# The first batch in two token halves, with its values mixed and transposed on chip, and experts run on one half while the other is prepared

**Chip, cores, metric.** One core of one Trainium2 chip. The metric is the device time of one execution in microseconds (us).

## The reference

A block attention feeds a mixture of four experts. What matters of it:

```python
# attention: q, k, v are [4, 8, 768, 64]; sort_net is [4, 8, 8, 8]
P = sort_net
for _ in range(5):                         # normalisation loop
    P = exp(P - P.max(-1)); P /= P.sum(-1); P /= P.sum(-2)
k_sorted = einsum('bhij,bhjcd->bhicd', P, k_blocks)      # mixes the 8 blocks of 96 tokens
v_sorted = einsum('bhij,bhjcd->bhicd', P, v_blocks)
attn = softmax(q_blocks @ k_sorted^T / 8);  attn_out = attn @ v_sorted   # within a block
# experts: x = attn_out as [3072, 512]; w1 [4, 512, 1024], w2 [4, 1024, 512]
p = domain_probs / domain_probs.sum(-1)
out = sum_e p[:, e] * (relu(x @ w1[e]) @ w2[e])
```

## The kernel before

Everything is fp16 for the matmuls. The 128 partitions of a loaded tensor hold 8 blocks x 16 tokens, so mixing the blocks is a matmul with a matrix built from the mixing weights and a mask (`PIk`, `PIv`). Mixed keys come out transposed, as scores need them. Mixed values come out with the wrong tokens on the partitions, and a trip through DRAM puts that right. Attention of batch b+1 is put as "filler" between the expert matmuls of batch b; attention of batch 0 runs alone, ahead of everything. Cut to what the change and the argument touch:

```python
for lo in range(0, H, 4):
    for nm in ("k", "v", "q"):
        load_natural(0, nm, lo, 4)                 # GpSimd queue, fp32 -> fp16
ident = const.tile([P, P], F16); make_identity(nc, ident)
nc.vector.tensor_reduce(eye16[:], ident..., AX.X, ALU.max)      # masks on VectorE
nc.vector.tensor_copy(maskk..., eye16...); nc.vector.tensor_copy(maskv..., eye16...)
...
load_w1(0); load_w2(0)
for it in range(5):                                # normalisation loop: ACT exp, then six DVE ops
    ...
nc.vector.tensor_copy(sn16[:], ...)                # broadcast, 1024 elements
for i in range(NB): nc.tensor.matmul(ps_R[:, i, :], sn16[:, i]..., ident[0:GH, 0:GH])
build_PI(nc.vector, 0, "v"); build_PI(nc.vector, 0, "k")
build_PI(nc.gpsimd, 1, "v"); build_PI(nc.gpsimd, 1, "k")
load_w1(1); load_w2(1)
for nm in ("k", "v", "q"): load_natural(1, nm, 0, H)
for n in range(2, GH // 4): build_PI(nc.gpsimd, n, "v"); build_PI(nc.gpsimd, n, "k")
for e in range(2, E): load_w1(e); load_w2(e)

def st_v(b, pr):                                   # mix the values of a head pair
    ...
    if pr % 2:                                     # after each four heads: through DRAM
        nc.sync.dma_start(vs_dram[b, qd]..., vo...)
        nc.sync.dma_start(vs..., vs_dram[b, qd]...)

for f in attention_order(0): f()                   # batch 0 alone
mix_weights()                                      # p_sb = p / sum(p), four DVE ops
for b in range(B):
    ...
    experts(b, attention_order(b + 1) if b + 1 < B else [])
```

The profiles name an instruction by the tiles that it writes and reads. Names that begin with `ps_` are tiles in PSUM: `ps_R` holds the mixing weights, `ps_k` and `ps_v` mixed keys and values (`ps_mk` and `ps_mv` in the changed kernel), `ps_q` transposed queries, `ps_s` scores, `ps_a` attention outputs with their row sums, `ps_x` these outputs transposed, `ps_h` and `ps_o` the first and second product of an expert. Their copies in SBUF are `kT`, `vo` (`vT` in the changed kernel), `qT`, `ET` (exponentials of the scores), `xsl` (normalised outputs), `xT` (input of the experts) and `hT`; `vs` are the values as attention needs them. In the changed kernel `ps_w` is the tile of the warm-up matmuls and also that of the transposed values.

Buffers in PSUM: two pools of two 4 KiB tiles. During batch 0 attention uses all four in turn; afterwards the experts have one pool and attention the other.

The softmax here doesn't subtract the row's maximum and nothing guards it: scores larger than these inputs give would overflow.

## Time and profile before

| | before |
|---|---|
| time, median (lowest to highest) | 431.98 us (431.8 to 432.4, 3 runs) |
| span of the profiled execution | 429.6 us |
| busy: PE / PEld / DVE / ACT / POOL | 387.3 / 212.8 / 155.4 / 128.3 / 35.1 us |
| first expert matmul on the chain | 56.79 us |
| one expert on one batch (64 + 48 matmuls) | 10.40 + 10.36 us |

PE is the TensorE, PEld its weight loads, DVE the VectorE, ACT the ScalarE, POOL the GpSimd. A PE that is 90% busy says little by itself; where the other 10% lies says more. The view of waits, for PE in the whole execution (engine, line, releaser, us in total, times, longest), puts it in two places, both at the start:

```profile
PE ps_R L158 <- DVE sn L152: 16.4, 1, 16.4
PE ps_a L288 <- DMA vs<-vs_dram: 16.2, 2, 15.7
```

The first is the wait for the normalisation loop, the second the wait for values that come back from DRAM. The prediction shows the chain and the timeline of this stretch.

### The profile page before, as it was taken

Reading aid. Unit: us, or ns where it says so; the run is one execution under the profiler, and the core shown is the slowest. Engines: PE = TensorE matmul, PEld = TensorE weight load, DVE = VectorE, ACT = ScalarE, POOL = GpSimd, SP = SyncE. Lnnn points to the kernel's source line nnn. Section 1 sums busy time; section 2 is a strip of 40 time slices with the busy share of each in tenths; the row PEclk is TensorE's granted clock in tenths of the full one; section 3 lists DMA queues with packets and bytes.
Section 4 is the critical chain, followed back from the end, with each engine's and each line's share of the span. In section 5 each row is a group of like instructions: output and inputs, shape, how many; then the busy total and the mean of one; then the engine's idle time right before and its main releaser. Section 6 shows DMA issues by size and latency. Waiting matters only on the chain.

```text
span 429.6 us, 6396 instructions
## 1 busy us (share of the span) xinstructions
PE 387.3 (90%) x2856; PEld 212.8 (50%) x2856; DVE 155.4 (36%) x265; ACT 128.3 (30%) x166; POOL 35.1 (8%) x51
## 2 busy tenths in 40 slices
PE   0321889999999999999999999999999999999995
PEld 0211655554646555555646454555556454545552
DVE  3831643434243434334253424343352403030312
ACT  1010323241605232351506041432406050514140
POOL 6396200000011000000000000000000000000000
PEclk9975569999999999999999999999999999999999
DMA  9999999940009422200000221200000300000003
GB/s 133 207 211 227 226 209 211 223 105 2 2 0 183 111 76 77 76 2 0 2 2 2 98 78 48 77 2 0 2 2 0 125 23 2 0 2 0 0 26 123
DMA packets 30027, 31.07 MB, mean 72 GB/s; under 512 B 1584, under 2 KB 24112, under 8 KB 30000
## 3 DMA queue, kind: packets, MB, share of 16 engines
q0 software_dynamic: 18800, 17.83, 25.5%
q1 hardware_dynamic: 11200, 12.84, 9.6%
q8 instruction: 22, 0.36, 0.3%
q14 instruction: 5, 0.04, 0.0%
HBM read 38.95 MB, written 9.54 MB: 113 GB/s over the span
## 4 chain that ended last, share of the span: by engine, by line
PE 86%; DMA 7%; DVE 4%; POOL 1%; issue 1%; ACT 0%; SPq 0%; POOLq 0%
PE ps_h L365 40%; PE ps_o L379 39%; DMA vs_dram<-vo 5%; PE ps_a L288 2%; DMA vs<-vs_dram 1%; PE ps_x L310 1%; PE ps_q L238 1%; PE ps_k L250 1%; PE ps_s L267 1%; PE ps_v L210 1%; DVE xsl L297 1%; DVE vo L217 0%; POOL nat_k L84 0%; POOL nat_v L84 0%; DVE PIk L173 0%
## 5 line engine op out<-in xcount | busy, mean ns | idle before, releaser
L365 PE MATMUL ps_h<-xT,w 128*128 128x384 f16 x1024 | 177.8, 329 | 0.0
L371 ACT ACTIVATE hT<-ps_h 128x768 f16<-128x768 f32 x128 | 103.8, 811 | 237.8 <-PE ps_h L365 237.8
L379 PE MATMUL ps_o<-w,hT 128*128 128x512 f16 x768 | 171.9, 379 | 0.0
L365 PEld LDWEIGHTS <-w 128*128 128x128 f16 x1024 | 97.9, 99 | 65.6 <-issue 2.2
L379 PEld LDWEIGHTS <-hT 128*128 128x128 f16 x768 | 73.6, 98 | 85.1
L390 DVE SCALAR_TENSOR_TENSOR oacc<-ps_o,p_sb,oacc 128x512 f32<-128x512 f32 x72 | 54.1, 751 | 104.9 <-PE ps_o L379 104.9
L274 ACT ACTIVATE ET<-ps_s 96x768 f16<-96x768 f32 x32 | 24.0, 802 | 37.8 <-PE ps_s L267 37.8
L386 DVE TENSOR_SCALAR oacc<-ps_o,p_sb 128x512 f32<-128x512 f32 x24 | 18.0, 751 | 34.5 <-PE ps_o L379 34.5
L288 PE MATMUL ps_a<-vs,ET 96*128 96x65 f16 x256 | 12.0, 206 | 16.2 <-DMA vs<-vs_dram 16.2
L297 DVE TENSOR_TENSOR xsl<-ps_a,rz 96x512 f16<-96x512 f32 x32 | 22.0, 687 | 1.1
L217 DVE CAST vo<-ps_v 128x768 f16<-128x768 f32 x16 | 15.1, 950 | 17.6 <-PE ps_v L210 17.6
L313 DVE COPY xT<-ps_x 128x768 f16<-128x768 f16 x16 | 8.9, 556 | 34.2 <-PE ps_x L310 34.2
L257 DVE CAST kT<-ps_k 128x768 f16<-128x768 f32 x16 | 15.2, 953 | 15.4 <-PE ps_k L250 15.2
L288 PEld LDWEIGHTS <-ET 96*128 96x128 f16 x256 | 11.1, 106 | 18.6 <-issue 16.0
L296 DVE RECIPROCAL rz<-ps_a 96x8 f32<-96x8 f32 x32 | 6.3, 197 | 34.3 <-PE ps_a L288 34.3
L242 DVE COPY qT<-ps_q 128x768 f16<-128x768 f16 x16 | 8.8, 551 | 19.3 <-PE ps_q L238 19.3
L158 PE MATMUL ps_R<-ident,sn 32*128 32x32 f16 x8 | 0.4, 185 | 16.4 <-DVE sn L152 16.4
L310 PE MATMUL ps_x<-ident,xsl 96*128 96x96 f16 x128 | 9.3, 224 | 3.6 <-DVE xsl L297 3.6
L84 POOL DMA_DIRECT2D nat_k<-in_k_dram x5 | 4.3, 868 | 85.9 <-PE ps_k L250 85.1
L310 PEld LDWEIGHTS <-xsl 96*128 96x128 f16 x128 | 7.9, 107 | 6.3 <-DVE xsl L297 4.4
L267 PE MATMUL ps_s<-qT,kT 64*128 64x96 f16 x256 | 9.5, 222 | 0.3 <-DVE kT L257 0.2
L210 PE MATMUL ps_v<-nat_v,PIv 128*128 128x384 f16 x32 | 8.8, 375 | 1.0 <-DVE PIv L180 1.0
(41 smaller groups left out, 89.2 us busy)
## 6 DMA issues: line engine op xcount, KB each, us to landing
w<-in_moe_w_dram POOLq DMA_DIRECT2D x8, 1024.0 KB, 20.9
out_dram<-oacc SPq DMA_DIRECT2D x24, 256.0 KB, 2.0
vs_dram<-vo SPq DMA_DIRECT2D x8, 396.0 KB, 6.5
vs<-vs_dram SPq DMA_DIRECT2D x8, 396.0 KB, 3.6
nat_k<-in_k_dram POOLq DMA_DIRECT2D x3, 768.0 KB, 23.3
nat_v<-in_v_dram POOLq DMA_DIRECT2D x3, 768.0 KB, 27.9
nat_q<-in_q_dram POOLq DMA_DIRECT2D x3, 768.0 KB, 30.7
nat_k<-in_k_dram POOLq DMA_DIRECT2D x2, 384.0 KB, 6.6
```

The lines of the kernel that those rows point to most:

```text
L217: nc.vector.tensor_copy(vo[:, :, ds(2 * (pr % 2), 2), 0:D], ps[:, :, 0:R * D].rearrange("p h (r d) -> p r h d", r=R),)
L257: nc.vector.tensor_copy(kT[:, 0:S].rearrange("p (i r c) -> p i r c", i=NB, r=R), ps.rearrange("p r (i c) -> p i r c", c=CP),)
L267: nc.tensor.matmul(pss[hh][:, i // HB, ds((i % HB) * BLK, BLK)], kT[ds(D * hh, D), ds(i * BLK, P)], qT[ds(D * hh, D), i, :], start=True, s ...
L274: nc.scalar.activation(ETs[2 * (pr % 2) + hh][:, 0:S].rearrange("c (a x) -> c a x", a=2), pss[hh][0:BLK, :, 0:HS], AF.Exp, bias=0.0, scale ...
L288: nc.tensor.matmul(ps[:, i // HB, ds((i % HB) * VW, D + 1)], ET[:, ds(i * BLK, P)], vs[:, i, 2 * (pr % 2) + hh, 0:D + 1], start=True, stop ...
L297: nc.vector.tensor_tensor(xsl[:, :, hh, :].rearrange("c (a i) d -> c a i d", a=2), av[:, :, :, 0:D], rz[:].broadcast_to([BLK, 2, HB, D]), ...
L310: nc.tensor.transpose(ps[:, i, :], xsl[:, i, :, :].rearrange("c h d -> c (h d)"), ident[0:BLK, 0:BLK])
L365: nc.tensor.matmul(ps[:, nh, 0:HS], w1sb[e][:, kc, ds(fc * P, P)], xT[:, kc, ds(nh * HS, HS)], start=(kc == 0), stop=(kc == NKC - 1),)
L371: nc.scalar.activation(hT[:, fc, :].rearrange("p (a x) -> p a x", a=2), ps[:, :, 0:HS], AF.Relu, bias=0.0, scale=1.0,)
L379: nc.tensor.matmul(ps[:], hT[:, fc, ds(r * P, P)], w2sb[e][:, fc, :], start=(fc == 0), stop=(fc == NFC - 1),)
L386: nc.vector.tensor_scalar(out=oacc[r][:], in0=ps[:], scalar1=pcol, scalar2=None, op0=ALU.mult)
L390: nc.vector.scalar_tensor_tensor(out=oacc[r][:], in0=ps[:], scalar=pcol, op0=ALU.mult, in1=oacc[r][:], op1=ALU.add,)
```

## The change

The intent is to shorten the stretch before the experts. Batch 0 is cut into two halves of 384 tokens (four of the eight blocks each). Only the first half is prepared ahead; its values are mixed into transposed form, copied out of PSUM, and turned by TensorE transposes (`h_w`) instead of by DRAM. (The functions `q_half`, `h_k`, `h_v`, `h_w`, `h_s`, `h_a` and `h_x` are the units of one half: queries, mixed keys, mixed values, transposed values, scores, attention outputs, transposed outputs.) The experts 0 and 1 then run on that half while the second half is prepared as filler. Smaller parts: masks and their reduction move to GpSimd, identity comes after two loads instead of six, 76 warm-up matmuls on the identity go before the loop's result is there, the broadcast copy is shared by DVE and ACT, and loads are reordered. The core of the diff:

```diff
-    for lo in range(0, H, 4):
-        for nm in ("k", "v", "q"):
-            load_natural(0, nm, lo, 4)
+    load_natural(0, "k", 0, 4)
+    load_natural(0, "q", 0, 4, 0, P // 2)          # 64 partitions = first half of q
     ident = const.tile([P, P], F16, name="ident")
     make_identity(nc, ident)
+    load_natural(0, "v", 0, 4)
+    load_natural(0, "k", 4, 4)
+    load_natural(0, "v", 4, 4)
+    load_natural(0, "q", 4, 4, 0, P // 2)
+    load_natural(0, "q", 0, H, P // 2, P // 2)
-    nc.vector.tensor_reduce(eye16[:], ident..., AX.X, ALU.max)
-    nc.vector.tensor_copy(maskk..., eye16...)
+    nc.gpsimd.tensor_copy(eye16[:], ident[:, 0:CP])
+    for j in range(1, NB):
+        nc.gpsimd.tensor_tensor(eye16[:], eye16[:], ident[:, ds(j * CP, CP)], ALU.add)
+    nc.gpsimd.tensor_copy(maskk..., eye16...)
 ...
+    warm(28)                                        # matmuls of the identity
+    for pr in range(2):
+        q_half(0, pr, 0, nc.scalar.copy)
+    warm(48)
 ...
+    def h_w(qd, hf):                                # values: transposes instead of DRAM
+        for n in range(2 * HB):
+            nc.tensor.transpose(ps[:, n, :], vT[:, ds(n * BLK, BLK)], ident[:])
+        nc.vector.tensor_copy(vs0s[qd]..., ps...)
 ...
-    for f in attention_order(0):
-        f()
+    h_k(0, 0); h_v(0, 0)                            # (first half, one call a line)
+    for pr in range(2, 4): q_half(0, pr, 0, nc.scalar.copy)
+    h_k(1, 0); h_s(0, 0); h_w(0, 0); h_v(1, 0)
+    ...
+    h_s(1, 0); h_a(0, 0); h_w(1, 0); h_x(0, 0, ...); h_a(1, 0); h_x(1, 0, ...)
     mix_weights()
+    second = [q_half 0, h_k 0, h_v 0, q_half 1, h_k 1, h_s 0, h_w 0, h_v 1,      # of half 1
+              q_half 2, h_a 0, q_half 3, h_w 1, h_s 1, h_x 0, h_a 1, h_x 1]
+    run([(0, 0, 0), (0, 1, 0)], second, 2)          # (batch, expert, half)
+    run([(0, 0, 1), (0, 1, 1), (0, 2, 0), (0, 2, 1), (0, 3, 0), (0, 3, 1)], attention_order(1))
+    for b in range(1, B):
+        ...
+        run([(b, e, None) for e in range(E)], attention_order(b + 1) if b + 1 < B else [])
```

## The prediction

> **What bounds the kernel now.** I read the busy slices of the page first (10.7 us each), then the chain that ended last in order of time, then the timeline of the first 60 us, then the DMA issues one by one.
>
> ```profile
> PE   0321889999999999999999999999999999999995
> PEclk9975569999999999999999999999999999999999
> DMA  9999999940009422200000221200000300000003
> ```
>
> From the sixth slice on the TensorE (PE) has no idle time; before it, it is mostly empty. The kernel is a start of some 56 us that waits for something else, and then one dense run of matmuls. The chain says the same:
>
> ```profile
> 20.96 13.06 DMA vs_dram<-vo
> 34.45 9.93 DMA vs_dram<-vo
> 44.40 5.91 DMA vs<-vs_dram
> ...
> 56.79 5.99 PE ps_h L365 x24
> ...
> 82.07 1.30 PE ps_h L365 x8
> 83.81 2.71 PE ps_h L365 x16
> ...
> 92.84 0.49 PE ps_a L288 x16
> ...
> 341.99 10.40 PE ps_h L365 x64
> ...
> 414.67 10.37 PE ps_o L379 x48
> 425.07 0.75 DVE oacc L390
> ```
>
> Columns: start, duration, what. The mixed values of batch 0 go to DRAM and back (vs_dram, vs); from 20.96 to 50.3 us this path is all that the chain holds. The first expert matmul that counts starts at 56.79, the last ends at 425.07: 368.3 us. One expert on one batch is 10.40 (ps_h, 64 matmuls) + 10.36 (ps_o, 48) = 20.76 us, so sixteen are 332.2. The other 36.1 us are attention work for batches 1 to 3 put between. The gap between two expert pieces gives a unit's price: 83.37 to 83.81, 0.44 us for the score matmuls of a head pair. By expert groups the four batches start at 56.79, 153.25, 247.62 and 341.99, so attention costs 94.4 - 83.0 = 11.3 us a batch; the first has 2.1 us more, because its first 24 matmuls took 5.99 us where later ones take 3.90: the TensorE was still at half clock. The end, 425.07 to 429.6, is 4.5 us; the measured time is 2.4 us above the span.
>
> The start itself, from the timeline:
>
> ```profile
> 2.40 0.26 ACT L140 ACTIVATE sn<-sn 32x64 f32<-32x64 f32 x1 [0.38 <-DMA sn<-in_sort_net_dram]
> 6.47 0.38 DVE L109 TENSOR_REDUCE eye<-ident 128x16 f16<-128x128 f16 x1 [6.47 <-POOL ident masks.py:199]
> 7.13 0.20 DVE L141 TENSOR_REDUCE srow<-sn 32x8 f32<-32x64 f32 x1
> 8.88 0.21 DVE L141 TENSOR_REDUCE srow<-sn 32x8 f32<-32x64 f32 x1 [0.32 <-ACT sn L140]
> 15.63 0.68 DVE L152 CAST sn<-sn 32x1024 f16<-32x1024 f32 x1
> 40.19 1.04 PE L288 MATMUL ps_a<-vs,ET 96*128 96x65 f16 x16 [15.69 <-DMA vs<-vs_dram]
> ```
>
> The first exponential of the normalisation loop is done at 2.66, but VectorE (DVE), in order, sits at the mask that needs the identity until 6.47, so the loop starts at 7.13 and ends at 15.6: 8.47 us for five rounds of 1.755.
>
> **What the Trainium skill says.** (1) "TensorE: Matmul & The Clock Gate", Part 1: The HAM clock gate: the array runs at half clock until about 3.4 us of sustained activity, and falls back after an idle window. The trace agrees where the granted clock shows it: 0.50 from 30 to 57 us, and the 5.99 against 3.90 us above. Its 1.00 for 16 to 24 us I don't believe: the four ps_v matmuls there (384 columns) stand 0.32 us apart, which is half speed. (2) "DMA: Bandwidth & Descriptors", Queues, rings and completion order: each DMA engine takes turns between queues packet by packet, so a store on the SyncE queue shares with weight loads. The trace agrees: the 396 KB store took 13.1 and 9.9 us while about 210 GB/s flowed, against a median of 6.5. (3) "PSUM — Partial Sum Buffer", Specifications: 8 banks of 2 KiB. Two pools of two 4 KiB tiles fill them, so attention units placed between experts have two buffers in turn; the trace of before has no such wait in its dense part, and the change places them more tightly.
>
> **The change part by part.**
>
> *Masks to GpSimd (POOL).* DVE is free when the exponential is done. The loop starts at 2.7 and ends at 2.7 + 8.5 = 11.2: 4.4 us earlier. The broadcast copy is halved over two engines: 0.4 instead of 0.68. Then four ps_R matmuls (0.3) and one 512-element product from PSUM (about 0.7): mixing can start near 12.6. The added warm-up matmuls lie before it in otherwise idle TensorE time; at full clock 48 of 128 columns cost 2.6 us, at half 5.1, so they end near 12 either way. Keys land at 6.2 and the rest of batch 0 by 15.9, as in before: each 384 KB load landed 1.95 us after the one ahead.
>
> *Half of batch 0 ahead of the experts, without DRAM.* The serial path, with rows of before for each copy: keys of four heads mixed on TensorE (24 short matmuls, 0.7) to 13.3; values to 14.0; ScalarE (ACT) evicts vT (0.81) to 14.9; q transposes; second keys to 15.6, evicted by DVE (0.95) to 16.6; scores from 15.6 to 16.2; exponentials (0.80 each), behind two q copies, to 17.8; value transposes 16.2 to 16.7, evicted by DVE (1024 f16, about 0.75 from 556 ns for 768) to 17.5; second values, ACT copy to 18.6; ps_a from 18.1; DVE two times 0.20 + 0.69 to 20.4; vs of the second four heads to 21.2; ps_a; again two normalisations to 23.5; transposes 0.45; ACT copy 0.81 to 24.8. So the dense run starts near 25.3 instead of 56.8. Weights of expert 0 are no earlier limit: w1 landed at 20.8 and w2 at 24.0 in before, after the same bytes. I add 1.0 us, half of the 2.1, for an even chance of a cold first stretch: 26.3.
>
> *The other half becomes filler.* By matmul count against units of before: four q halves (0.3 each) 1.3, four mixings of 24 matmuls (0.75) 3.0, two value transposes 0.7, two scores 0.9, two ps_a 1.0, two ps_x 0.7: 7.5 us of TensorE time, moved into the dense run, not removed.
>
> *Waits of these fillers.* Sixteen units go into twelve slots of 1.3 to 1.7 us, with two buffers. Scores directly after a key mixing wait for its 0.95 us eviction: 1.0. ps_a directly after a q half waits for an accumulation (0.75) and the q copy: 0.9. ps_x directly after scores waits for ACT (a relu and an exponential): 1.2. Others 0.9. Sum 4.0. Batch 1 has its 24 units in 38 slots instead of 50: 0.6.
>
> *Expert work.* Halves use 384 columns as before; matmul count and price stay: 332.2. Attention of batches 1 to 3: 33.9.
>
> Sum: 26.3 + 332.2 + 7.5 + 4.0 + 0.6 + 33.9 + 4.5 = 409.0 us of span; plus 2.4 is 411.4 us. I say **411**, 4.9% below 432.0. In differences: -30.5 for the start, -2.1 for the cold stretch counted inside it, +7.5 for the moved work, +4.6 for waits.
>
> **The rivals.** *The loads become the bound.* At about 200 GB/s, batch 0 and four weight matrices are landed by about 32 us, batch 1 by 44, the last weights by about 62. Expert 1 needs its first matrix at about 40, batch 1's attention starts near 59, expert 2 near 87. All have 8 us or more in hand, so I give this 10%; it would make the time 415 to 422. *The store and load of batch 1's values starve ps_a.* The bounce still exists there. It starts near 62 us, ps_a follows some 24 us later; even the 19 us of the contended first bounce fits. If not, +5. *TensorE stays cold through the start*: at half clock each short unit on the path costs 0.2 to 0.3 us more, some 2 us, and the first experts 2 us: 414. *Fillers stall harder*: if every unit of batch 0's second half waits about 1 us, waits are 12 instead of 4: 419. *Better*: if fillers overlap with evictions as smoothly as in before, and the start is at 24: 405.
>
> **Range and chances.** The start may be 2.5 us off either way, the filler waits -3 to +6; together 404 to 419 for 8 in 10. To lose the 2% (423.3) most of the rivals would have to come together: faster 0.95, same 0.04, slower 0.01.
>
> **What would show it.** First dense ps_h near 25 us; no DMA in the chain before it, but alternating PE, ACT and DVE; the normalisation loop ending near 11.2; TensorE idle 3 to 6 us between 26 and 60 us, released by DVE and ACT; each full batch 94 us apart afterwards, and the same 4.5 us end. I am wrong if weights release the first ps_h, if the dense run starts after 30, or if idle TensorE time after the start is above 10 us.

## More of the kernel before

Times are medians of several executions. The experiments were run in three sets on three chips, the kernel before in each of them (432.10, 431.86 and 431.29 us), so the figure to compare between sets is the ratio to the kernel before.

## The result, and the profile after

The changed kernel takes 414.99 us (414.46 to 416.58, 4 runs) against 432.13 (431.8 to 432.4, 4 runs) in the same rounds: ratio 0.961, 95% interval 0.9582 to 0.9638, faster. Ratios here and below are the mean time of one kernel's runs over that of the other's of the same rounds, so not quite the ratio of the medians that are quoted. The output is correct.

| us | before | after |
|---|---|---|
| span | 429.6 | 412.6 |
| busy PE / DVE / ACT / POOL | 387.3 / 155.4 / 128.3 / 35.1 | 395.3 / 154.2 / 135.6 / 36.5 |
| first dense expert matmul, on the chain | 56.79 | 30.15 |
| last expert matmul ends | 425.07 | 408.90 |

The busy slices of the page (10.3 us each) for the changed kernel:

```profile
PE   5679989999999999999999999999999999999996
PEclk9959999999999999999999999999999999999999
DMA  9999999930079412000001222000000300000003
```

The empty stretch has shrunk from some five slices to three. The third digit of the clock is a 5: by the record the TensorE runs at half clock (the clock granted to it, as a share of the full one, is 0.5) in the later part of the preparation of batch 0's first half. The chain that ended last, in order of time, has no transfer of values in it any more, but one load:

```profile
5.52 10.84 DMA nat_q<-in_q_dram
...
17.35 0.58 PE ps_mk L388 x24
17.96 0.97 DVE kT L394
18.97 0.76 PE ps_s L423 x15
...
29.30 0.81 ACT xT L459
30.15 2.08 PE ps_h L514 x6
...
62.32 1.30 PE ps_h L514 x8
...
137.08 1.30 PE ps_h L498 x8
...
325.82 10.40 PE ps_h L498 x64
...
398.50 10.37 PE ps_o L528 x48
408.90 0.75 DVE oacc L539
```

From these starts the time splits up. Experts 0 and 1 on the first half, with the second half of batch 0 as filler, take 62.32 - 30.15 = 32.17 us, of which 20.76 are expert matmuls, so the filler costs 11.4 us. The other six half experts with batch 1 as filler take 74.76 us, 62.28 of them expert work, so 12.5 for batch 1. The next two batches take 94.37 us each, as before, and the last 83.08. The end takes 3.7 instead of 4.5 us.

The waits of PE between 29 and 62 us in the changed kernel:

```profile
PE ps_x L456 <- ACT ET L430: 1.1, 1, 1.1
PE ps_s L423 <- DVE kT L394: 0.9, 1, 0.9
PE ps_a L444 <- DVE qT L182: 0.5, 1, 0.5
```

They are the three waits that the prediction named (1.2, 1.0, 0.9), and there is only 0.2 us besides, the wait of the first expert matmul at 30.15 for its input `xT`, which belongs to the start. Three lines of the timeline (start, duration, engine, what, idle time before) show things that it did not name:

```profile
8.48 4.58 PE L168 MATMUL ps_w<-ident 128*128 128x128 f16 x48
...
13.00 0.26 PE L216 MATMUL ps_R<-ident,sn 32*128 32x32 f16 x4
...
28.58 3.23 DVE L482 TENSOR_SCALAR den<-den 128x24 f32<-128x24 f32 x1
```

The inputs of `ps_R` were ready at 12.0 us, but it stands behind the warm-ups. A VectorE instruction on 24 elements takes 3.23 us, where the kernel before had 0.18. And the busy times in stretches of 2 us (stretch, length, busy time of each engine with instruction counts, granted clock, DMA share, GB/s) date the fall of the clock:

```profile
18.00:20.00 2.00, 1.10 (x19) 0.88 (x18) 0.92 (x1) 0.25 (x1) 0.00 (x0) 0.74 1.12 213
20.00:22.00 2.00, 1.47 (x32) 1.38 (x30) 1.02 (x2) 1.26 (x2) 0.01 (x1) 0.50 1.14 204
```

The record has 1.00 before and again from about 32.6 us. For the first 12 us it isn't to be believed, as the prediction said of the kernel before: the first 28 warm-ups took 3.17 us, 113 ns each, where in a later run 30 took 1.83 us, 61 ns each.

### The profile page after: what moved, and what is told of

Same layout as the page of the kernel before. It is cut to its first block, busy times and chain, and to the rows that moved or that the text cites. A ratio compares the mean times of both kernels' runs of the same rounds, so it can differ in the third digit from the quotient of the medians.

```text
span 412.6 us, 7014 instructions
## 1 busy us (share of the span) xinstructions
PE 395.3 (96%) x3148; PEld 221.1 (54%) x3148; DVE 154.2 (37%) x259; ACT 135.6 (33%) x177; POOL 36.5 (9%) x63
## 4 chain that ended last, share of the span: by engine, by line
PE 91%; DVE 3%; DMA 3%; ACT 1%; POOL 1%; issue 1%; ACTq 0%; POOLq 0%
PE ps_o L528 41%; PE ps_h L498 31%; PE ps_h L514 10%; DMA nat_q<-in_q_dram 3%; DVE xsl L339 2%; PE ps_s L322 1%; PE ps_q L293 1%; PE ps_k L305 1%; PE ps_a L354 1%; PE ps_x L368 1%; PE ps_v L265 1%; PE ps_x L456 1%; ACT ET L430 1%; PE ps_s L423 0%; DVE kT L394 0%
## 5 line engine op out<-in xcount | busy, mean ns | idle before, releaser
L504 ACT ACTIVATE hT_None<-ps_h 128x768 f16<-128x768 f32 x96 | 77.9, 811 | 156.6 <-PE ps_h L498 156.6
L528 PE MATMUL ps_o<-w,hT_None 128*128 128x512 f16 x576 | 128.3, 379 | 0.0
L528 PEld LDWEIGHTS <-hT_None 128*128 128x128 f16 x576 | 55.5, 98 | 64.6
L520 ACT ACTIVATE hT<-ps_h 128x768 f16<-128x768 f32 x32 | 26.0, 811 | 62.4 <-PE ps_h L514 62.4
L528 PE MATMUL ps_o<-w,hT 128*128 128x512 f16 x192 | 44.5, 380 | 0.0
L514 PEld LDWEIGHTS <-w 128*128 128x128 f16 x256 | 24.1, 99 | 16.2 <-issue 1.5
L528 PEld LDWEIGHTS <-hT 128*128 128x128 f16 x192 | 17.6, 98 | 19.7 <-ACT hT L520 0.3
L329 ACT ACTIVATE ET<-ps_s 96x768 f16<-96x768 f32 x24 | 18.0, 802 | 21.3 <-PE ps_s L322 21.3
L312 DVE CAST kT<-ps_k 128x768 f16<-128x768 f32 x12 | 11.4, 954 | 13.4 <-PE ps_k L305 13.4
L272 DVE CAST vo<-ps_v 128x768 f16<-128x768 f32 x12 | 11.4, 954 | 7.5 <-PE ps_v L265 7.5
L168 PE MATMUL ps_w<-ident 128*128 128x128 f16 x76 | 7.8, 295 | 3.4 <-POOL ident masks.py:199 3.4
L238 POOL TENSOR_TENSOR PIk<-maskk,Rs 128x512 f16<-128x512 f16 x6 | 6.3, 1053 | 45.9 <-PE ps_k L305 45.9
L168 PEld LDWEIGHTS <-ident 128*128 128x128 f16 x76 | 7.3, 139 | 3.5 <-POOL ident masks.py:199 3.4
```

What stands on the lines that cost most here:

```text
L168: nc.tensor.matmul(ps[:, m % 4, :], ident[:], ident[:], start=True, stop=True)
L272: nc.vector.tensor_copy(vo[:, :, ds(2 * (pr % 2), 2), 0:D], ps[:, :, 0:R * D].rearrange("p h (r d) -> p r h d", r=R),)
L312: nc.vector.tensor_copy(kT[:, 0:S].rearrange("p (i r c) -> p i r c", i=NB, r=R), ps.rearrange("p r (i c) -> p i r c", c=CP),)
L329: nc.scalar.activation(ETs[2 * (pr % 2) + hh][:, 0:S].rearrange("c (a x) -> c a x", a=2), pss[hh][0:BLK, :, 0:HS], AF.Exp, bias=0.0, scale ...
L504: nc.scalar.activation(hT[:, fc, :].rearrange("p (a x) -> p a x", a=2), ps[:, :, 0:HS], AF.Relu, bias=0.0, scale=1.0,)
L514: nc.tensor.matmul(ps[:, a, 0:HS], w1sb[e][:, kc, ds((2 * f2 + a) * P, P)], xT0[hf][:, :, kc, :], start=(kc == 0), stop=(kc == NKC - 1),)
```

## The experiments

**Theory.** Most of the 17 us come from taking the contended trip through DRAM off the chain; the earlier loop adds a few. Overlapping experts with the second half adds little, because that work only moves into a TensorE that is full. **Rivals.** The overlap is the main source; or the trip could have been mended more simply.

### Where the 17 us come from

Four kernels undo one part of the change, or do one part alone in the kernel before.

**The loop late again** (changed kernel; the reduction and the keys' mask on DVE, identity after all loads; the values' mask, needed later, stays on GpSimd):

```diff
-    ident = ...; make_identity(nc, ident)           # after two loads
+    ident = ...; make_identity(nc, ident)           # after all loads of batch 0
-    nc.gpsimd...                                    # masks on GpSimd
+    nc.vector.tensor_reduce(eye16[:], ...); nc.vector.tensor_copy(maskk..., ...)
```

> The changed kernel with the start of the normalisation loop as it was: masks on VectorE, identity made after all the loads of batch 0 are issued. The loop should again start near 7.1 us and end near 15.6 instead of 11.4. Theory (the early loop is worth little by itself, because in the changed kernel ps_R waited for the warm-up matmuls until 13.0 and the second q transposes waited for their load until 16.4): the dense run starts only 2 to 3 us later, 417 to 418 us. Rival (the loop is the head of the serial chain and its whole shift is paid): 4.2 us later, 419 us.

Measured: 418.16 us, ratio to before 0.9684 (0.9665 to 0.9703). The broadcast copies came 4.6 us later (15.97 instead of 11.40), `ps_R` 3.4 us (16.44 instead of 13.00), and on the chain the experts began 3.3 us later than at 30.15:

```profile
33.45 2.08 PE ps_h L512 x6
```

So about 3.2 us of the gain belong to the early loop here, a little more than the theory said and less than the full shift. About 1.1 us of the shift was hidden behind the warm-ups. PE no longer waits for the second q load in this run.

**The whole of batch 0 ahead of the experts** (changed kernel; the same operations, no filler beside experts 0 and 1 on the first half):

```diff
+    for f in second:
+        f()
     mix_weights()
...
-    run([(0, 0, 0), (0, 1, 0)], second, 2)
+    run([(0, 0, 0), (0, 1, 0)], [], 2)
```

(The product for the second half is built before it, too.)

> The changed kernel with the second half of batch 0 prepared before the experts instead of between their matmuls; all operations are the same. Theory A (the gain is mostly the removal of the trip through DRAM): the second half costs about 13 us serially, but takes its 11.4 us out of the dense run, so the time grows by 1 to 4 us, to 416 to 419. Theory B (running experts on one half while the other is prepared is the main source): it grows by 10 us or more, to 425 or above.

Measured: 417.45 us, ratio 0.9671 (0.9645 to 0.9696). The chain reaches the experts 11.4 us later,

```profile
41.55 7.52 PE ps_h L514 x32
```

and gets 9.1 of them back by the start of batch 1's filler (65.77 instead of 63.46). Theory A's range held: running experts beside the second half is worth about 2.5 us of the 17. That the rest is the removal of the trip, as theory A also says, this run alone doesn't show.

**Masks on GpSimd alone, in the kernel before:**

```diff
-    nc.vector.tensor_reduce(eye16[:], ...); nc.vector.tensor_copy(maskk...); nc.vector.tensor_copy(maskv...)
+    nc.gpsimd.tensor_copy(eye16[:], ident[:, 0:CP]); (7 x nc.gpsimd.tensor_tensor add)
+    nc.gpsimd.tensor_copy(maskk..., ...); nc.gpsimd.tensor_copy(maskv..., ...)
```

> The kernel before with only the masks built on GpSimd. The loop should start at about 2.8 us and end at 11.3. If the start is a chain that moves along as a whole: the store of the values begins 4.3 us earlier and the time falls by about 4 us, to 428. If the trip through DRAM ends when the queued weight loads let it (rival): under 1.5 us gained.

Measured: 426.79 us, ratio 0.9883 (0.9863 to 0.9902). The loop ended at 11.2, the store began at 16.7 instead of 20.96, and the chain reached the experts 4.2 us earlier than at 56.79:

```profile
52.63 6.62 PE ps_h L367 x24
```

The chain moved as a whole; the interval (1.2% faster) excludes no effect.

**Competing loads held back, in the kernel before:**

```diff
     build_PI(nc.gpsimd, 1, "k")
-    load_w1(1); load_w2(1)
-    for nm in ("k", "v", "q"): load_natural(1, nm, 0, H)
     for n in range(2, GH // 4): ...                 # 12 us of GpSimd work
+    for nm in ("v", "k", "q"): load_natural(1, nm, 0, H)
+    load_w1(1); load_w2(1)
```

> The kernel before with the loads that compete with the trip through DRAM held back: the products for the later batches come first on GpSimd, then batch 1 (v, k, q), then the weights of expert 1. If most of the 29 us between the first store and the last load of the values is contention with loads: each 396 KB transfer falls to 4 to 7 us, the dense run starts near 45 instead of 57 us, and the time falls by 8 to 12 us, to 420 to 424, unless batch 1's values now come late. If the trip itself is slow: under 4 us gained.

Measured: 422.91 us, ratio 0.979 (0.9775 to 0.9805). The chain:

```profile
20.96 7.01 DMA vs_dram<-vo
27.99 3.43 DMA vs<-vs_dram
...
47.90 5.52 PE ps_h L365 x24
```

The store took 7.0 instead of 13.1 us and the load 3.4; the experts began 8.9 us earlier. PE waited for the values for 7.0 us instead of 16.2: more than half of the trip's cost was contention. Moving four lines, and loading the values of batch 1 first, gives more than half of what the whole change gives; the interval lies far from no effect.

**Both edits, in the kernel before** (the two diffs above together):

> The kernel before with both single edits of the first set: masks on GpSimd (-5.3 us alone) and the competing loads held back (-9.2 us alone). The values still go through DRAM and batch 0 is not halved. If the two act on different stretches of the same chain, they add: about 417.6 us, 2.6 us behind the changed kernel. If the earlier store meets the weight loads of expert 0 again, which land at 24 us: 420 to 422.

Measured: 421.24 us, ratio 0.9758 (0.974 to 0.9776). The two didn't add: -5.3 and -9.2 alone, -10.6 together. The earlier store met the weight loads of expert 0, as the second alternative said:

```profile
16.78 10.60 DMA vs_dram<-vo
```

It ended 0.6 us sooner than the store of the run before, which began 4.2 us later. So rearranging what stands around the trip gives 10.6 of the 17 us, and some 6.4 us (ratios 0.9758 and 0.961) are left to everything else in the change; the overlap with experts is about 2.5 of them by the run above. No run takes only the trip away, with batch 0 whole and nothing else changed, so what that part is worth by itself is not shown.

### Why the start was longer than predicted

**The q loads and transposes ahead of the loop's end:**

```diff
-    load_natural(0, "q", 0, 4, 0, P // 2)
+    load_natural(0, "q", 0, H, 0, P // 2)
-    load_natural(0, "q", 4, 4, 0, P // 2)
...
-    for pr in range(2): q_half(0, pr, 0, nc.scalar.copy)
-    warm(48)
+    for pr in range(4): q_half(0, pr, 0, nc.scalar.copy)
+    warm(34)
...
-    for pr in range(2, 4): q_half(0, pr, 0, nc.scalar.copy)     # between the mixings
```

> The changed kernel with the first q half of all eight heads loaded second and transposed before the loop ends, so that no q transpose stands between the first and second key mixings (34 warm-up matmuls instead of 48 keep ps_R where it was). Theory (the wait for the q load until 16.4 us and the two q copies on ScalarE lay on the serial path): second keys are mixed by 16 instead of 17.9 us, the dense run starts 2 to 2.8 us earlier, about 412.5 us. Rival (the path then waits for the first keys' copy or for the exponentials anyway): under 0.7 us gained.

Measured: 414.49 us, ratio 0.9601 (0.9587 to 0.9615): no difference from the changed kernel that the intervals resolve. In the trace the second keys were mixed by 17.2 instead of 17.9 us and the experts began 1.0 us sooner (29.11). But `ps_R` slipped to 13.67, because the larger q load landed at 9.1 and the 34 warm-ups ran mostly at half clock (92 ns each); and the full clock came back 0.8 us later (about 33.4 instead of 32.6 us), so that the stretch to batch 1's filler took 0.8 us more (32.93 against 32.17). The q load did leave the path, but for 1.0 us and not for 2 to 2.8, and the later full clock gave most of that away.

**Fewer warm-ups:** `warm(48)` becomes `warm(36)`.

> The changed kernel with 36 instead of 48 warm-up matmuls in the second block. The sums for ps_R were ready at 12.0 us but ps_R started at 13.0, behind the last warm-ups. Theory (the warm-ups delay the path): ps_R starts near 12.0, but the q load at 16.4 still holds the path, so at most 0.5 us is gained: 414.5 to 415. Rival (the twelve warm-ups are what brings the full clock): the clock stays half through the first mixings and the time grows by 1 to 3 us.

Measured: 414.83 us, ratio 0.9606 (0.9588 to 0.9623): within the theory's range, but not told apart from no effect. The chain again began with the q load (landed at 16.4), so this wait hid the earlier `ps_R`. But the sign that the rival named did come in the profiled execution. Its page (10.3 us a slice) has

```profile
PEclk9558999999999999999999999999999999999999
```

and finer windows give 0.50 from 10.0 to 33.9 us: the first keys were mixed in 0.86 instead of 0.57 us, and the experts began at 30.67, 0.5 us later than in the changed kernel. Whether the twelve warm-ups made this is not shown: the clock had been full early (the 24 q transposes at 8.5 us took 0.56 us, against 0.85 in the changed kernel) and was lost during the warm-ups themselves.

**Keep the TensorE occupied in the first half of batch 0:** 80 dummies on the identity (14 matmuls, 66 transposes), each put ahead of the real work of a unit, in that unit's PSUM tile.

```diff
+    DUM = {("q", 2, 0): 18, ("s", 0, 0): 14, ("w", 0, 0): 8, ("x", 0, 0): 10, ("x", 1, 0): 30}
     # in h_s, and in the same way with transposes in q_half, h_w and h_x:
+        for m in range(DUM.get(("s", qd, hf), 0)):
+            nc.tensor.matmul(pss[0][:, m % 2, 0:P], ident[:], ident[:], start=True, stop=True)
```

> The changed kernel with 80 matmuls and transposes of the identity put where TensorE waited in the first half of batch 0 (their outputs are overwritten by the real ones), so that the results stay the same. Theory (the clock fell to half at 19 us because TensorE had too little to do, which lengthened each unit on the path and the first experts): the granted clock stays at 1.0 from 13 us on and 2 to 3 us are gained, about 412.5. Rivals: transposes don't count as activity and the clock falls as before (within 0.5 us of 415), or the added work delays the path (above 415).

Measured: 413.74 us, ratio 0.9577 (0.956 to 0.9594). The clock line of its page, and a wait of PE in its first 64 us:

```profile
PEclk9999999999999999999999999999999999999999
...
PE ps_mv L391 <- DVE qT L185: 1.0, 1, 1.0
```

The clock held, and the experts began at 28.42, 1.7 us sooner. But the gain in time is only some 1.3 us by the medians, with intervals that overlap slightly, since a new wait of 1.0 came up: the first copy of the fillers stood on DVE behind the instruction on `den` that now took 4.21 us.

**The small VectorE instructions moved:** `mix_weights()` goes from the end of the first half to the wait for `ps_R`.

```diff
+    (body of mix_weights)                           # after the broadcast copy
     ps_R = psM.tile(...)
...
-    mix_weights()
```

First in the changed kernel:

> The changed kernel with the four small VectorE instructions that normalise p_sb moved from the end of the first half to the wait for ps_R near 12 us, when GpSimd runs no elementwise work. The tensor_scalar among them took 3.23 us there (0.18 in the kernel before), while GpSimd built products. Theory (it was held up by GpSimd's work, and nothing on TensorE waited for it): it takes 0.2 us at the new place and the time stays within 0.7 us of 415.0. Rival (the first fillers waited for it unseen): 1 us or more gained.

Measured: 414.89 us, ratio 0.9621 (0.9596 to 0.9647), the same as the changed kernel. The instruction:

```profile
12.06 0.33 DVE L213 TENSOR_SCALAR den<-den 128x24 f32<-128x24 f32 x1
```

So it was long because of where it stood, and nothing paid for it there. Then in the keep-warm kernel:

> The keep-warm kernel (413.7) with the same move. There the first q copy stood behind a tensor_scalar of 4.21 us and TensorE waited 1.0 us for it. Theory: that wait goes and about 1 us is gained, 412.4 to 413. Rival (the wait is replaced by one for another buffer): no gain.

Measured: 413.1 us, ratio 0.9584 (0.9558 to 0.961), not told apart from the keep-warm kernel's 0.9577. In the trace the wait of 1.0 us is gone (29.10 to 60.18 is 31.1 us, against 32.15), but this execution began the experts 0.7 us later, its `ps_R` at 13.48 instead of 12.79. The mechanism is seen in the trace; its worth in time stays open.

**All of it, with one unbroken warm-up** (keep-warm, moved instructions, q first, and `warm(56)` ... `warm(30)` instead of `warm(28)` ... `warm(48)`):

> The same with the q halves moved ahead (as in the q-first run) and the warm-ups made one unbroken stretch (56, then 30 after the q transposes). Theory (the full clock comes only after an unbroken stretch, so it should now come before 10.5 us, ps_R should start by 12.3 and the path should be 1.5 to 2 us shorter than in the keep-warm run): dense run from about 26.7 us, about 411 us. Rival (the clock still rises at 12.5 us or later): ps_R starts at 13 or later and the time is 412.5 or above.

Measured: 410.09 us, ratio 0.9504 (0.9486 to 0.9522), clearly below the changed kernel. From the timeline:

```profile
3.49 5.33 PE L168 MATMUL ps_w<-ident 128*128 128x128 f16 x56 [3.49 <-POOL ident masks.py:199]
...
12.14 0.26 PE L224 MATMUL ps_R<-ident,sn 32*128 32x32 f16 x4
```

The 30 warm-ups after the q transposes took 1.83 us, about 61 ns each: full clock before 10.5 us (and 1.84 us in the next kernel, which starts alike). That only an unbroken stretch can bring it, as the theory says, is not so: in the run with fewer warm-ups it was full by 8.5 us after 28 warm-ups and a gap of 1.95 us. `ps_R` began at 12.14 and the experts at 27.77 instead of 30.15. The clock still fell, from about 14.6 to 18.0 us, because PE was busy for only 0.36 us between 12 and 14; the moved `den` instructions also held the product of the first half until 13.3.

**Another order of the second half's units:**

```diff
-  ... q_half 1, h_k 1, h_s 0, h_w 0, h_v 1, q_half 2, h_a 0, q_half 3, h_w 1, h_s 1, h_x 0, h_a 1, h_x 1
+  ... h_k 1, q_half 1, h_w 0, h_s 0, h_v 1, q_half 2, q_half 3, h_a 0, h_w 1, h_x 0, h_s 1, h_a 1, h_x 1
```

> The same with another order of the sixteen units of batch 0's second half, so that no scores follow directly on a key mixing, no ps_a on a q half and no ps_x on scores. In the changed kernel TensorE waited 0.9 + 0.5 + 1.1 us at these places. Theory (they are waits for the two buffers of the attention pool): 1.2 to 2 us less than the run before it, 409 to 410. Rival (each wait moves to the next unit): within 0.5 us.

Measured: 408.64 us, ratio 0.9475 (0.9454 to 0.9495). The intervals of this and the last kernel overlap slightly, so take the trace with it: from the first dense matmul (28.98) to

```profile
57.85 1.30 PE ps_h L521 x8
```

are 28.87 us, against 31.07 in the kernel before it; of the waits between units one of 0.5 us is left. In this profiled execution the clock stayed half until about 21.7 us and the start was 1.2 us later, with the same code up to there. This is the best version: 1.5% below the run with only the `den` instructions moved (414.89, same rounds), which equals the changed kernel, and 5.3% below the kernel before.

All twelve other kernels, like the changed one, gave correct results.

## Why the prediction was right

It said 411 (404 to 419), faster with 0.95. Measured 414.99: in the range, with the mechanism as told. But the start lay outside its own range of 2.5 us either way, and one of its signs of being wrong came, by a hair: a dense run that starts after 30 us (30.15). Another sign failed too: the chain before the dense run does hold a DMA, the q load (5.52 to 16.36). The total stayed inside its range because that was wide, and because the filler, its waits and the cold stretch together (11.4 for 12.5) and the end came out some 2 us smaller than said; that part is luck. Its sum, term by term, in us of span:

| term of the prediction | predicted | measured |
|---|---|---|
| start of the dense run | 25.3 | 30.15 |
| half of a cold first stretch | 1.0 | about 1.1, inside the next line |
| units of the second half, and their waits | 7.5 + 4.0 | 11.4, with the cold stretch |
| experts | 332.2 | 332.2 |
| batch 1 as filler | 11.3 + 0.6 | 12.5 |
| batches 2 and 3 | 22.6 | 22.7 |
| end | 4.5 | 3.7 |
| span | 409.0 | 412.6 |

- **The trip through DRAM leaves the chain, and experts start some 30 us sooner.** Right: 26.6 us sooner. The runs add how this divides. Held-back loads alone gave 9.2 us and early masks alone 5.3, but both together only 10.6. The other 6.4 came only with values kept on chip and batch 0 halved, which no run takes apart further than the 2.5 for the overlap.
- **The second half's work is moved, not removed.** Right: 11.4 us of filler appeared (about 1.1 of it the cold clock), and the run without overlap showed that the overlap nets only 2.5 us.
- **The three named waits.** Right in place, and together 2.5 us of the 3.1 given to them; for the 0.9 given to "others" the view shows nothing. The reordered run shows that they were a matter of order.
- **Batch 1 and its values.** No wait for a load or for the trip of batch 1's values appears after 30 us. The rival of late loads did not come true for weights; it did for q, see below.
- **The size that was off is the start: 25.3 predicted, 30.15 measured.** Step by step, with delays handed on: mixing began at 14.3 instead of 12.6 (1.0 of it the warm-ups that I put at "near 12", the rest the copies and the product). The second keys were mixed at 17.9 instead of 15.6, now 2.3 behind: I had the q loads landing "as in before", but the one that the second q transposes need landed at 16.4, after two loads that are needed later. Scores of the first keys ended at 19.7 instead of 16.2, 3.5 behind, because half of them need the PSUM tile that the second keys leave; the prediction had overlooked this wait for a tile. By the code, `ps_R` keeps one of the two tiles of its pool until its second half is copied at 21.4 us, so that the second q transposes, the second keys, half of the first scores and the second values pass through the one other tile in turn; the waits of 0.4, 0.9 and 0.5 us for `qT`, `kT` and `ET` between 17 and 21.3 us fit this. No run copies `ps_R` earlier. `ps_a` began at 22.9 instead of 18.1, 4.7 behind: another wait for a tile (0.5), and TensorE at half clock. From there on the delay stayed near 4.9.
- **The cold TensorE**, a rival put at 2 us for the start and 2 for the first experts, came true in part (the prediction put the time at 414 for this case): the keep-warm run began experts 1.7 us sooner, and the moved-instruction version of it needed 1.1 us less in the first stretch than the changed kernel.

The delays of single steps at the start are read from one trace; the experiments confirm the clock and the order of q together (the unbroken warm-up run), not each tenth of a microsecond.

## What to carry to other kernels

When an engine is full for most of the time, work that is overlapped with it is moved and not saved; count what a change takes off the path ahead of the full stretch, and charge what it puts into that stretch. Before replacing a slow transfer, see what shares the queues with it: here a reordering of loads gave half of the gain. And in a short serial start, check three things for each step: when its load lands in the order of issue, which tile it must wait for, and whether the TensorE will still have its clock.

## What the Trainium skill lacked or had wrong

- **"TensorE: Matmul & The Clock Gate", Part 1: The HAM clock gate.** Its rule is to have no idle gaps above some 3.4 us. In the changed kernel the clock fell to half at about 19 us although no wait of PE between 13 and 19 us was longer than 1.2 us; by the record PE was busy for 2.7 of these 6 us. With dummies (4.1 of the 6 us) it held. So short waits are enough to lose it; the page says as much of another kernel, but gives no share of activity that would keep it. That the window's phase differs from run to run agrees with the page: with the same start, two kernels were at half clock until 18.0 and until 21.7 us. The runs add that the clock is lost in whole steps: in all twelve traces that have such a stretch, each one recorded at half clock lasts a multiple of 3.41 us (3.4 and 6.8 in these two, 13.6 in the changed kernel, 34.1 in the kernel before).
- **The same page, Part 4: PE-mode transpose**, says that transposes don't count as activity in the same way. In the keep-warm run all dummies after 18.7 us were transposes (48 of them), and the clock stayed at 1.0 where it was at 0.5 without them. That doesn't decide it: 14 dummy matmuls and 18 transposes had come before 19 us, when the clock was lost without them, and real matmuls ran between. No run leaves out these 48 alone or uses transposes alone.
- **"SBUF — State Buffer", SBUF: two separate sides**, says that the loser of the port pair shared by VectorE and GpSimd waits for the other's whole instruction. The tensor_scalar on 128x24 took 3.23 us (4.21 in the keep-warm run) beside GpSimd products of 1.05 us each that followed one another, and 0.33 us away from them. If it is this lock, it was lost to three or four instructions in a row, not to one, which the page does not warn of.
- **"DMA: Bandwidth & Descriptors", Anatomy of one DMA**, fits 2.0 us plus bytes / 436e3. The loads that convert fp32 to fp16 ran at about 200 GB/s of written bytes (384 KB every 1.95 us in the kernel before), and a 396 KB store took from 3.6 us (median in the changed kernel) to 13.1 us (the first one in the kernel before, among the loads). No page gives the rate of a converting load.
